# Moving loads and turns of u, v and z in the opening couples of a fused attention and maxout kernel

## The chip, the cores and the metric

The kernel runs on one core of one Trainium2 chip. A core has a matrix engine (TensorE, PE in the profile, with its weight loads as PEld), three more compute engines (VectorE or DVE, ScalarE or ACT, GpSimd or POOL), and SyncE (SP), which here only issues DMAs. Each engine runs its own queue of instructions in order, and they wait for one another through semaphores. The metric is the device time of one execution in microseconds (us), lower is better. Five executions of the kernel before took 918.5, 917.55, 910.27, 917.88 and 922.46 us; the median is 917.88.

## The reference: what is computed

There are 8 batches of 3072 positions. u and v have 256 columns, z has 64. The output of the first half, flattened to 24576 rows, feeds the second half:

```python
scores = (1.0 / S) * z @ z.T            # per batch, S = 3072
attn = np.maximum(scores, 0.0) ** 2
x = u * (attn @ v)
h1, h2 = x @ w1, x @ w2                 # 256 -> 1024
out = np.maximum(h1, h2) @ w_out        # 1024 -> 256
```

The scores are symmetric, so a block of them on one side of the diagonal is the transpose of a block on the other side.

## The kernel before

**Tiling.** A batch is cut into 6 groups of 512 positions (g), so its scores are 6 x 6 blocks of 512 x 512. Two groups make a couple (c = 0, 1, 2), and all couples of all batches are counted by i: couples 0 to 2 are batch 0, 3 to 5 are batch 1. v and z come in pieces of two groups, written v(batch, piece) and z(batch, piece); u comes by group, u(batch, group).

**Scores and their transposes.** `score_pair` computes a block in two halves: matmuls of zT (L211), a relu on ScalarE into r_sb (L224) and a square on VectorE (L230, L232). Blocks on the diagonal are computed as triangles and completed by three DMA transposes (L235). Blocks below the diagonal are made by `mirror`, one DMA transpose of a whole block (L263). During the steps of a couple the scores of the next couple are computed; the squares are issued 8 steps after their matmuls.

**Attention.** A couple is a list of steps, each with two matmuls of 64 rows that run side by side (L892). From couple 3 on it is a fast matrix product with 7 instead of 8 block products: VectorE forms S1, S2 and S3 of score blocks (L331, L335, L339, in `prepare`), S4 (L782), and combinations of v (`combine_v`, L171 to L174). Couple 2 is computed plainly. An accumulator that changes from one half of the array to the other needs a relay: a nop that waits for the last matmul of the old half and releases the first of the new one. In the plain couple relays are on GpSimd's queue, in the others on ScalarE's.

**Gate and feed-forward.** After the steps of couple i comes `second(i - 1)`: the feed-forward of the couple before (`ff`, L440 to L476), with tasks of VectorE hung between its matmuls: the gates of couple i (`gate`, L424, which reads uT), then S1, S2, S3 for couple i + 1. S2 is used from the first steps of the next couple, S3 from its step 12.

**Transfers.** `load_v`, `load_u` and `load_z` issue on GpSimd (L157, L183, L135) and cast to bf16. `turn_u` is a DMA transpose on SP (L187) of an un tile into uT; `turn_z` makes two copies on VectorE (L142) and a DMA transpose on SP into zT (L143). There are two buffers each of un, uT, zn and zd, so the third load of u must wait for the first turn. Five buffers hold v, so v(1,2) takes the buffer of v(0,2) and waits until couple 2, which reads v(0,2) first, is done with it after 32 steps. zT has four places; z(2,0) takes the one of z(0,2).

**Order of the work.** The program is written in order by hand. For each couple `plan` lists (step, what, batch, number). At that step the transfer is put into its engine's queue; a step is no time in itself, only a place in the order. At a step the relays come first, then squares that are due (with their triangles and mirrors), mirrors that are ready, scores, and then the entries of the plan. In the lists of couple 2:

```python
(1, turn_u, 0, 4), (2, load_v, 1, 0), (4, turn_u, 0, 5),
(6, load_v, 1, 1), (34, load_v, 1, 2),
```

Of the kernel before, what the change touches and what calls it, by code (L numbers as in the profile page):

```python
# [11 lines left out]
def kernel(  # L12
# [541 lines left out]
    with tc.manual_schedule():  # L554
# [185 lines left out]
        for i in range(PLAIN // 2, len(couples)):  # L740
# [98 lines left out]
            if i == 2:  # L839
                plan = [  # L840
                    (1, turn_u, 0, 4),
                    (2, load_v, 1, 0),
                    (4, turn_u, 0, 5),
                    (6, load_v, 1, 1),
                    (34, load_v, 1, 2),
                ]
            if i == 3:
                plan = [
                    (2, load_u, 1, 0),
                    (6, load_u, 1, 1),  # L850
                    (22, load_z, 2, 0),
                    (26, load_z, 2, 1),
                    (36, turn_u, 1, 0),
                    (42, turn_u, 1, 1),
                    (len(steps), load_u, 1, 2),
                    (len(steps), load_u, 1, 3),
                ]
            if i == 4:
                plan = [x for x in plan if x[1] not in (load_z, turn_z)] + [
                    (2, turn_z, 2, 0),  # L860
                    (10, turn_z, 2, 1),
                    (14, load_z, 2, 2),
                    (44, turn_z, 2, 2),
                ]
# [91 lines left out]
```

## Time and profile before

| | us |
|---|---|
| median of five executions | 917.88 |
| the profiled execution | 918.5 |
| its span, first to last instruction | 916.7 |
| TensorE busy | 901.5 |
| VectorE busy | 722.0 |
| ScalarE busy | 602.6 |
| GpSimd busy | 105.9 |

The mean granted clock of TensorE was 0.996 of full speed. The page of the profile gives busy times by engine, a picture of the span in 40 slices, the DMA queues and the chain of work that ended last. Further views answer for a stretch of time: the timeline of one engine, the waits (who waited for whom), and the busy times by stretch. A row of a timeline has start, duration, engine, line of the kernel, operation, output <- input, and how many of them were merged; in brackets stands the idle time before it and what ended it. "SPq" is the queue of SP; its duration is the time that a transfer's issue took there, not the transfer. Matmuls run in a pipeline, so their rows overlap.

### The profile page before, as it was taken

To read this page: it belongs to the slowest core of one execution; us is meant where nothing else is said; L and a number is where in the kernel's file an instruction comes from. 1 tells how busy PE (TensorE), PEld (TensorE's weight loads), DVE (VectorE), ACT (ScalarE), POOL (GpSimd) and SP (SyncE) were. 2 spreads that over 40 slices of the span, in tenths; PEclk is the share of its full clock that TensorE was granted. 3 is DMA by queue.
4 is the path that set the end of the run, shared out by engine and by line. 5 is a ranking of instruction groups with operands and counts; after the bars stand their busy time and mean duration, and the time that the engine had idled before them with its cause. 6 is when DMAs were issued, how large, how long until landed. Compare 5 with 4: busy or idle time off the path is not lost.

```text
span 916.7 us, 19227 instructions
## 1 busy us (share of the span) xinstructions
PE 901.5 (98%) x7478; PEld 520.1 (57%) x7526; DVE 722.0 (79%) x1091; ACT 602.6 (66%) x1193; POOL 105.9 (12%) x199
## 2 busy tenths in 40 slices
PE   8899999999999999999999999999989999999998
PEld 4356465665565655665646656556455564655655
DVE  6572689778997799887997979979789788995640
ACT  7687967567666676667676666666756667673445
POOL 4101010110101111101011012010110110100000
PEclk9899999999999999999999999999999999999999
DMA  9999978989798996999979999799999989987201
GB/s 182 174 190 187 196 160 143 188 164 192 142 177 156 158 202 113 202 149 180 170 127 205 148 159 182 144 193 155 154 154 133 189 159 182 166 161 149 74 24 70
DMA packets 381580, 145.60 MB, mean 159 GB/s; under 512 B 360240, under 2 KB 364720, under 8 KB 381488
## 3 DMA queue, kind: packets, MB, share of 16 engines
q1 hardware_dynamic: 359040, 91.79, 62.4%
q0 software_dynamic: 22448, 52.57, 30.9%
q8 instruction: 59, 0.97, 0.5%
q14 instruction: 33, 0.27, 0.1%
HBM read 59.77 MB, written 25.17 MB: 93 GB/s over the span
## 4 chain that ended last, share of the span: by engine, by line
PE 92%; DMA 3%; DVE 2%; issue 1%; ACT 1%; POOL 0%; ACTq 0%; DVEq 0%; POOLq 0%
PE acc L892 43%; PE o_ps L463 18%; PE d_ps L440 17%; PE s_ps L211 7%; PE o_ps L454 4%; PE acc L279 3%; DMA v_sb<-in_v_dram 2%; DMA blk<-blk 1%; DVE blk L232 1%; DMA uT<-un 0%; ACT r_sb L224 0%; PE acc L582 0%; DVE blk L335 0%; DVE blk L331 0%; PE w2o_ps L671 0%
## 5 line engine op out<-in xcount | busy, mean ns | idle before, releaser
L892 PE MATMUL acc<-blk,v_sb 64*128 64x512 bf16 x2208 | 451.3, 376 | 0.0
L224 ACT ACTIVATE r_sb<-s_ps 128x512 bf16<-128x512 f32 (+3 forms) x672 | 336.0, 559 | 128.1 <-PE s_ps L211 84.3
L892 PE MATMUL acc<-blk,vt 64*128 64x512 bf16 x1512 | 364.9, 376 | 2.5 <-DVE blk L335 2.3
L892 PEld LDWEIGHTS <-v_sb 64*128 64x128 bf16 x2208 | 176.2, 94 | 137.5 <-issue 10.0
L232 DVE TENSOR_TENSOR blk<-r_sb 128x1024 bf16<-128x1024 bf16 x257 | 172.7, 689 | 93.8 <-ACT r_sb L224 93.1
L447 ACT ACTIVATE g_sb<-d_ps 128x512 bf16<-128x512 f32 x384 | 193.3, 631 | 28.2 <-PE acc L892 17.8
L463 PE MATMUL o_ps<-w_out_sb,g_sb 128*128 128x256 bf16 x1536 | 175.5, 273 | 0.0
L892 PEld LDWEIGHTS <-vt 64*128 64x128 bf16 x1512 | 139.3, 94 | 62.7
L440 PE MATMUL d_ps<-xT,w_sb 128*128 128x512 bf16 x720 | 167.9, 380 | 2.8 <-ACT g_sb L447 0.2
L463 PEld LDWEIGHTS <-g_sb 128*128 128x128 bf16 x1536 | 150.3, 98 | 17.4
L475 ACT COPY o_sb<-o_ps 128x512 f32<-128x512 f32 (+1 forms) x98 | 56.3, 577 | 133.2 <-PE o_ps L463 131.5
L767 DVE TENSOR_TENSOR h_sb<-h_sb,acc 128x512 f32<-128x512 f32 x168 | 109.6, 684 | 28.3 <-ACT h_sb L771 20.9
L211 PE MATMUL s_ps<-zT 64*128 64x512 bf16 (+3 forms) x676 | 126.7, 359 | 0.7 <-ACT zT L129 0.4
L440 PEld LDWEIGHTS <-w_sb 128*128 128x128 bf16 x768 | 73.3, 98 | 89.8 <-issue 10.5
L476 POOL DMA_DIRECT2D out_dram<-o_sb x88 | 48.0, 546 | 524.4 <-ACT o_sb L475 524.4
L335 DVE TENSOR_TENSOR blk<-blk,blk 128x2048 bf16<-128x2048 bf16 x63 | 77.2, 1225 | 2.2
L331 DVE TENSOR_TENSOR blk<-blk,blk 128x2048 bf16<-128x2048 bf16 x63 | 76.8, 1220 | 0.0
L782 DVE TENSOR_TENSOR blk<-blk,blk 128x2048 bf16<-128x2048 bf16 x63 | 76.7, 1220 | 0.0
L339 DVE TENSOR_TENSOR blk<-blk,blk 128x2048 bf16<-128x2048 bf16 x63 | 73.3, 1220 | 4.1 <-DMA blk<-blk 4.1
L424 DVE SCALAR_TENSOR_TENSOR xT<-h_sb,uT 128x512 bf16<-128x512 f32 x96 | 62.1, 686 | 3.8 <-PE o_ps L454 3.8
L230 DVE TENSOR_TENSOR blk<-r_sb 128x512 bf16<-128x512 bf16 (+3 forms) x162 | 46.3, 324 | 19.9 <-ACT r_sb L224 18.9
L211 PEld LDWEIGHTS <-zT 64*128 64x128 bf16 x676 | 36.2, 95 | 38.6 <-DVE zT L129 0.9
(47 smaller groups left out, 317.5 us busy)
## 6 DMA issues: line engine op xcount, KB each, us to landing
out_dram<-o_sb POOLq DMA_DIRECT2D x88, 256.0 KB, 3.7
un<-in_u_dram POOLq DMA_DIRECT2D x48, 256.0 KB, 5.9
v_sb<-in_v_dram POOLq DMA_DIRECT2D x21, 512.0 KB, 7.7
blk<-blk SPq DMA_TRANSPOSE x240, 4.8
zn<-in_z_dram POOLq DMA_DIRECT2D x21, 128.0 KB, 4.8
v_sb<-in_v_dram POOLq DMA_DIRECT2D x6, 256.0 KB, 7.1
out_dram<-o_sb SPq DMA_DIRECT2D x6, 256.0 KB, 2.0
blk<-in_moe_w_dram POOLq DMA_DIRECT2D x2, 512.0 KB, 8.2
```

The lines of the kernel that those rows point to most:

```text
L211: nc.tensor.matmul(s_ps[h][:, lo[h] :], zT[rows, z_at(b, blk * G + tiles[h]), :], zT[rows, q + lo[h] // P : q + G, :].rearrange("p t c -> ...
L224: nc.scalar.activation(o, s, AF.Relu)
L232: nc.vector.tensor_mul(a[:, k : k + 2, :], r, r)
L331: nc.vector.tensor_add(*alike(f["S1"], f["A21"], f["A22"]))
L335: nc.vector.tensor_sub(*alike(f["S2"], f["S1"], f["A11"]))
L339: nc.vector.tensor_sub(*alike(f["S3"], f["A11"], f["A21"]))
L440: nc.tensor.matmul(d_ps, w15_sb[:, kc, ts(nb, P)], xT[:, kc, :], start=(kc == 0), stop=(kc == KD - 1),)
L447: nc.scalar.activation(g_sb[:, nb, :], d_ps, AF.Relu)
L463: nc.tensor.matmul(o_ps[t // 2][:, t % 2, :], g_sb[:, nb, ts(t, P)], w_out_sb[:, nb, :], start=False, stop=(nb == KF - 1 and t % 2 == 1),)
L767: nc.vector.tensor_add(out, a, b_)
L782: nc.vector.tensor_sub(f["A12"].ap, f["A12"].ap, f["S2"].ap)
L892: mm = nc.tensor.matmul(a.out(acc[name]), w()[rows], a.moving(rows, j), start=name not in opened, stop=left[name] == 0,)
```

## The change

Three lists of the plan are edited; nothing else. In couple 2 the three loads of v(1) move from steps 2, 6 and 34 to 12, 16 and 36. In couple 3 the loads of z(2,0) and z(2,1) move from steps 22 and 26 to 14 and 18, and the turns of u(1,0) and u(1,1) from 36 and 42 to 22 and 26. The turn of z(2,0) moves from step 2 of couple 4 to step 66 of couple 3. A couple of the fast kind has 84 steps, the plain one 96.

```diff
             if i == 2:
                 plan = [
                     (1, turn_u, 0, 4),
-                    (2, load_v, 1, 0),
                     (4, turn_u, 0, 5),
-                    (6, load_v, 1, 1),
-                    (34, load_v, 1, 2),
+                    (12, load_v, 1, 0),
+                    (16, load_v, 1, 1),
+                    (36, load_v, 1, 2),
                 ]
             if i == 3:
                 plan = [
                     (2, load_u, 1, 0),
                     (6, load_u, 1, 1),
-                    (22, load_z, 2, 0),
-                    (26, load_z, 2, 1),
-                    (36, turn_u, 1, 0),
-                    (42, turn_u, 1, 1),
+                    (14, load_z, 2, 0),
+                    (18, load_z, 2, 1),
+                    (22, turn_u, 1, 0),
+                    (26, turn_u, 1, 1),
+                    (66, turn_z, 2, 0),
                     (len(steps), load_u, 1, 2),
                     (len(steps), load_u, 1, 3),
                 ]
             if i == 4:
                 plan = [x for x in plan if x[1] not in (load_z, turn_z)] + [
-                    (2, turn_z, 2, 0),
                     (10, turn_z, 2, 1),
                     (14, load_z, 2, 2),
                     (44, turn_z, 2, 2),
```

## The prediction

> **What bounds the kernel now.** I began with the page. Its busy line says that TensorE works nearly all the time:
>
> ```profile
> PE 901.5 (98%) x7478; PEld 520.1 (57%) x7526; DVE 722.0 (79%) x1091; ACT 602.6 (66%) x1193; POOL 105.9 (12%) x199
> ```
>
> The chain that ended last agrees (PE 92%, DMA 3%). An average can hide a slow stage, so I cut the span at the first d_ps matmul of each feed-forward (the list of the chain gives 111.70, 148.55, 185.00 and so on) and asked for busy times by stretch. Columns: stretch, its length, busy us (and instructions) of PE, PEld, DVE, ACT, POOL, then the TensorE clock, DMA share, GB/s.
>
> ```profile
> 30.00:40.00 10.00, 6.51 (x56) 2.97 (x53) 6.52 (x12) 6.23 (x12) 1.81 (x3) 0.95 1.45 153
> 40.00:50.00 10.00, 9.97 (x68) 4.50 (x69) 4.20 (x8) 6.11 (x12) 0.00 (x0) 0.71 1.33 199
> ...
> 90.00:100.00 10.00, 10.00 (x96) 4.55 (x94) 6.03 (x9) 9.37 (x18) 0.53 (x1) 1.00 1.24 207
> ```
>
> ```profile
> 111.70:148.55 36.85, 36.74 (x307) 20.89 (x309) 34.20 (x54) 25.12 (x51) 4.87 (x9) 1.00 0.73 146
> 148.55:185.00 36.45, 36.35 (x306) 22.57 (x308) 30.94 (x53) 23.23 (x49) 4.86 (x9) 1.00 1.02 184
> ...
> 222.00:258.70 36.70, 36.59 (x307) 20.97 (x309) 34.81 (x59) 24.50 (x49) 4.33 (x8) 1.00 0.82 149
> 258.70:295.15 36.45, 36.34 (x307) 22.58 (x309) 30.37 (x50) 23.23 (x49) 4.35 (x8) 1.00 0.95 172
> ...
> 662.00:702.70 40.70, 38.10 (x309) 21.86 (x311) 35.40 (x59) 24.43 (x50) 4.34 (x8) 1.00 1.11 143
> ```
>
> The change edits couples 2, 3 and 4 (i = 2, 3, 4; some 86 to 185 us). Couple 2 runs from 85.7 to 111.7, x96 matmuls in the row 90:100 and as many in 100:110; the timeline there shows pairs of matmuls starting every 0.216 us without a gap. Couple 3, with the feed-forward before it, is 111.70:148.55, and couple 4 is 148.55:185.00. The same two couples of the next batch take 36.70 and 36.45. So couple 3 is 0.15 us over its twin, couple 4 is level, and I find no wait of TensorE between 72 and 662 us over 0.4 us. What is lost at all is lost elsewhere: near 35 us (3.5 us idle, then a clock of 0.71) and at 662:702 (4.0 us over its twin, 36.70). The change touches neither. **The gain open to it in this execution is about 0.2 us.** The question is what it can spoil.
>
> **The queues that it reorders.** A step number orders an instruction only within its own engine's queue. SP's queue (start, time in the queue, line, transfer), couple 3 and the end of it:
>
> ```profile
> 136.00 4.45 SPq L235 DMA_TRANSPOSE blk<-blk  x3
> 140.54 1.45 SPq L187 DMA_TRANSPOSE uT<-un  x1
> 142.08 3.78 SPq L235 DMA_TRANSPOSE blk<-blk  x3
> 146.38 3.09 SPq L263 DMA_TRANSPOSE blk<-blk  x1
> 149.57 1.25 SPq L187 DMA_TRANSPOSE uT<-un  x1
> 150.92 10.71 SPq L263 DMA_TRANSPOSE blk<-blk  x3
> ```
>
> L235 are the triangles, L263 the mirrors, L187 the turns of u. GpSimd's queue:
>
> ```profile
> 87.24 1.10 POOL L157 DMA_DIRECT2D v_sb<-in_v_dram  x2
> 95.58 0.53 POOL L157 DMA_DIRECT2D v_sb<-in_v_dram  x1 [7.24 <-PE s_ps L211]
> 128.72 1.10 POOL L183 DMA_DIRECT2D un<-in_u_dram  x2
> 129.78 1.10 POOL L135 DMA_DIRECT2D zn<-in_z_dram  x2
> 144.49 0.53 POOL L183 DMA_DIRECT2D un<-in_u_dram  x1 [13.60 <-DMA uT<-un]
> 153.40 0.53 POOL L183 DMA_DIRECT2D un<-in_u_dram  x1 [8.38 <-DMA uT<-un]
> ```
>
> And VectorE, which consumes what they bring:
>
> ```profile
> 154.03 1.28 DVE L424 SCALAR_TENSOR_TENSOR xT<-h_sb,uT 128x512 bf16<-128x512 f32 x2
> 155.23 1.22 DVE L331 TENSOR_TENSOR blk<-blk,blk 128x2048 bf16<-128x2048 bf16 x1
> ...
> 161.25 3.50 DVE L339 TENSOR_TENSOR blk<-blk,blk 128x2048 bf16<-128x2048 bf16 x3 [1.15 <-DMA blk<-blk]
> 164.67 0.49 DVE L142 COPY zd<-zn 128x512 bf16<-128x512 bf16 x2
> ```
>
> **Part 1, loads of v(1) later in couple 2.** In this plain couple the relays ("half done" nops) sit on GpSimd's queue and wait for TensorE, so here a step number is a time. Step 0 starts at 85.67; four steps and a score pair take 1.08 us. Relays of step 12 wait for the end of step 11, about 88.9; the load follows, so v(1,0) goes out near 89.0 instead of 87.24 and v(1,1) near 90.1 instead of 87.79; v(1,2) near 96.6 instead of 95.58. Before, they landed 7.5 to 9.6 us after issue, the last at about 103.6. The first reader is L171 at 118.0 on VectorE. With the slowest landing of any v in this trace (14.0 us) the last would land at 110.6. Nobody is late. A load holds GpSimd 0.53 to 0.55 us, the next relays come four steps (0.9 to 1.1 us) later and are needed another four steps on: no wait is added. The Trainium skill speaks against this part: "DMA: Bandwidth & Descriptors", Rules for kernel authors, says to issue a transfer early and wait for it late. If its cover were gone, later issue would cost what it is later, 1.0 to 2.3 us; by the row, with more than 7 us of cover left, 0. I take 0. What is gained, that the turns of u(0,4) and u(0,5) do not share their time with v (they landed in 10.5 and 12.2 us here, against 3.1 to 3.4 in couple 3), ends at 103.1 and is read by L424 at 113.2: also 0.
>
> **Part 2, loads of z(2) from 22, 26 to 14, 18.** GpSimd's order is u, u, z, z before and after, with nothing of couple 3 between (its relays are on ScalarE). The rows show z issued at 129.78, long before step 22 (132.7). No change: 0.
>
> **Part 3, turns of u(1,0), u(1,1) from 36, 42 to 22, 26.** Each costs SP 1.25 to 1.45 us of queue. The mirror of block (2,3) is emitted at step 15 and runs 132.68 to 135.9; the first triangle is emitted at 27, the second at 39. So the turns pass both triangles and one mirror. The loads of u land 4.6 to 5.4 us after 128.7, by 134.7, before SP comes free, so the turns do not block it. New order: turns 136.0 to 138.8, first triangle 138.8 to 143.2 (2.8 us later), second 143.2 to 147.1 (1.3 later), mirrors from there as before or 0.5 earlier, since the turn at 149.57 is gone. Who waits for triangles: S1 of the own blocks, L331 at 155.23. The second triangle's last piece landed by 149.3 (issue 144.6 plus 4.7), now by 150.6; cover shrinks from 5.9 to 4.6 us. Cost 0. Gain: uT(1,1) landed at 152.9 for a gate at 154.03, a cover of 1.15 us that becomes some 12; the third and fourth loads of u, held at 144.49 and 153.40 until a turn freed a buffer, go out near 140 and 141.5, in the stretch 140:150, where the DMA share is 0.69. Nothing waited there, so 0.
>
> **Part 4, turn of z(2,0) from step 2 of couple 4 to step 66 of couple 3.** Two copies of 287 ns leave VectorE at 164.67 (0.49 us together) and come near 144.5, where it is busy without a break; one transpose (1.3 us of SP) passes the mirrors flushed at the couple's end. The mirrors issued from 152.92 on move 0.7 us back; the last to matter landed at 161.25, when the first S3 (L339) began. TensorE uses S3 from step 12 of couple 4, 166.9, while the first L339 ends at 162.5: 4.4 us of cover, 4.2 for the third. Copies plus transpose eat 0.5 to 1.2 of it. The other end of VectorE's 0.49: ScalarE had already waited 1.38 us on L232 at 143.3 (three buffers of r_sb), so a score could be late by up to 0.5; TensorE showed nothing of the 1.38, so I take 0 and keep +0.5. In return the zT of batch 2, landed 170.9 and first read at 174.3, gains 20 us of cover.
>
> **Sum.** Against the profiled execution, 918.5 us (span 916.7 and 1.8 around it): parts 0, 0, 0 and 0, within -0.2 and +0.5; about 918.4. The median of the five runs, 917.88, lies 0.6 below that execution, so **917.8**.
>
> **Rivals.**
> A, all of it is hidden: 917.8, chance 0.88. That part of the change does nothing (the loads of z) belongs here.
> B, slower: the mirrors behind the moved turn of z land too late for S3. It decides when they slip by more than 4.2 us beyond 161.25. For: SP's transposes can swell, a turn in couple 2 held the queue 5.56 us and landed in 10.5 to 12.2. With u and z swollen so, the slip is 7.1 (10.5 - 3.4) + 1.3 - 4.2 = 4.2 us of stall. Then the clock: the Trainium skill ("TensorE: Matmul & The Clock Gate", Part 1: The HAM clock gate) says an idle window of about 3.4 us halves the clock and about as much busy time restores it, so 1.7 us more. The row says worse: 0.71 over 40:50 is 5.8 us at half, 2.9 us lost. By the rule 923.7, by the row 924.9; I use the row. Against: in 130 to 150 the DMAs land in 2.3 to 5.7 us and the share is under 0.9. Chance 0.08, half of it over 1% only with a disturbance on top.
> C, faster: the thin covers (1.15 us of uT, 3.4 of zT) are overdrawn in other executions than the one profiled, or the stretch 662:702 falls differently with shifted transfers. Worth up to 4.0 there, and 3.5 + 2.9 if the early stall went too: 911.5 to 914. Against: the change is far from both places. Chance 0.04.
>
> **Range and chances.** The runs before spread from 910.27 to 922.46, so a median of a few may move by 3 or 4 us unprovoked; 1% (9.2 us) is about what a measurement can tell from no change. 911.5 (C) to 924.0 (most of B). Faster 0.03, same 0.92, slower 0.05.
>
> **What would show it.** v_sb issues at 89, 90 and 96.6; the z loads still right behind u near 130; SP with two L187 ahead of the first L235, and L143 before the last L263s; first L235 2.8 us later; uT gates unhindered; stages still 36.7 and 36.45. I am wrong if TensorE waits for L335 or L339 near 164 to 170 us, for zT, or if the clock falls below 1.00 after 86 us.

## The result, and the profile after

The change moves nothing that can be measured: the ratio of after to before is **1.0004, 95% interval 0.9980 to 1.0028**. The medians are 919.89 us over 43 executions after (910.56 to 939.75) and 922.26 us over 80 executions before (909.8 to 948.82). The ratio compares only the executions within 1.5% of the fastest of each kernel and the medians take all of them, which is why the two do not agree to the last 0.3%.

The profiled execution after took 920.89 us, its span is 919.1. Busy times by stretch, cut at the start of the first d_ps matmul of each feed-forward, 0.44 us ahead of the marks in the prediction, which leaves the lengths as they are (stretch, length, busy us and instructions of PE, PEld, DVE, ACT, POOL, then TensorE clock, DMA share, GB/s). The rows are couple 2, couple 3, couple 4, and the first couple of batch 4:

```profile
64.32:114.06 49.74, 44.12 (x349) 22.72 (x348) 17.94 (x29) 35.24 (x68) 4.90 (x9) 0.93 1.18 192
114.06:150.92 36.86, 36.76 (x309) 20.91 (x309) 34.28 (x56) 25.57 (x52) 5.40 (x10) 1.00 0.78 142
150.92:187.37 36.45, 36.35 (x308) 22.56 (x309) 30.44 (x51) 23.23 (x49) 4.33 (x8) 1.00 0.95 176
444.66:484.40 39.74, 37.63 (x309) 21.63 (x309) 34.90 (x58) 24.29 (x49) 4.35 (x8) 1.00 1.12 149
```

Couples 3 and 4, which hold five of the eight moved entries, take 36.86 and 36.45 us, what they took before within 0.01 us. Couple 2 took 49.74 where an execution without a wait takes 41.97 (below). TensorE's timeline there shows the reason:

```profile
86.77 0.38 PE L211 MATMUL s_ps<-zT 64*128 64x512 bf16 x2
86.98 1.03 PE L892 MATMUL acc<-blk,v_sb 64*128 64x512 bf16 x8
93.32 0.61 PE L211 MATMUL s_ps<-zT 64*128 64x512 bf16 x2 [5.31 <-DMA zT<-zd]
```

A score of batch 1 waited 5.31 us for a turn of z(1), and the clock fell for a while (0.93 over the stretch). That turn is not one of those moved. Its transpose came late to SP, behind a mirror:

```profile
73.87 9.50 SPq L263 DMA_TRANSPOSE blk<-blk  x1
83.46 2.41 SPq L143 DMA_TRANSPOSE zT<-zd  x1
```

It went out 19.1 us after the mark of the feed-forward; in an execution without a wait (sp_only, below) it was 12.0. The obvious suspect is the change itself, which puts the loads of v beside these turns later. But a kernel whose program up to couple 3 is that of before (z20_late, below) waited at the same place:

```profile
91.96 0.61 PE L211 MATMUL s_ps<-zT 64*128 64x512 bf16 x2 [4.52 <-DMA zT<-zd]
```

There the turn had reached SP after 12.6 us, hardly later than in sp_only, and was late all the same. The first couple of batch 4 has the other loss, 39.74 us where 36.68 is the time without a wait: VectorE waits for v, as it did near 662 us in the profile before. Its waits over 447 to 485 us:

```profile
DVE vt L171 <- DMA v_sb<-in_v_dram: 3.1, 1, 3.1
```

SP's queue after, couple 3 and the end of it (start, time in the queue):

```profile
138.94 2.64 SPq L187 DMA_TRANSPOSE uT<-un  x2
141.67 9.07 SPq L235 DMA_TRANSPOSE blk<-blk  x6
150.84 7.58 SPq L263 DMA_TRANSPOSE blk<-blk  x3
158.53 1.93 SPq L143 DMA_TRANSPOSE zT<-zd  x1
160.55 3.92 SPq L263 DMA_TRANSPOSE blk<-blk  x1
```

Both turns of u stand ahead of both triangles. The turn of z (L143) passes one mirror; three of the four that follow the triangles are still ahead of it. GpSimd's queue:

```profile
84.82 0.54 POOL L157 DMA_DIRECT2D v_sb<-in_v_dram  x1 [2.53 <-PE s_ps L211]
85.90 0.54 POOL L157 DMA_DIRECT2D v_sb<-in_v_dram  x1 [0.54 <-PE acc L892]
98.90 0.53 POOL L157 DMA_DIRECT2D v_sb<-in_v_dram  x1 [12.45 <-PE s_ps L211]
...
131.54 1.10 POOL L183 DMA_DIRECT2D un<-in_u_dram  x2
132.60 1.10 POOL L135 DMA_DIRECT2D zn<-in_z_dram  x2
144.34 0.53 POOL L183 DMA_DIRECT2D un<-in_u_dram  x1 [10.64 <-DMA uT<-un]
146.05 0.53 POOL L183 DMA_DIRECT2D un<-in_u_dram  x1 [1.17 <-DMA uT<-un]
```

The loads of v now wait for TensorE through the relays; the loads of z(2) follow u at once, exactly as before; the third and fourth loads of u lie 1.7 us apart instead of 8.9.

### The profile page after: what moved, and what is told of

It is laid out like the page before. It is cut to its first block, busy times and chain, and to the rows that moved or that the text cites. A ratio compares the mean times of both kernels' runs of the same rounds, so it can differ in the third digit from the quotient of the medians.

```text
span 919.1 us, 19229 instructions
## 1 busy us (share of the span) xinstructions
PE 901.7 (98%) x7478; PEld 520.3 (57%) x7526; DVE 721.7 (79%) x1091; ACT 602.4 (66%) x1193; POOL 105.4 (11%) x199
## 4 chain that ended last, share of the span: by engine, by line
PE 90%; DMA 5%; DVE 2%; issue 2%; ACT 1%; POOL 0%; ACTq 0%; POOLq 0%; DVEq 0%
PE acc L892 42%; PE o_ps L463 17%; PE d_ps L440 17%; PE s_ps L211 6%; PE o_ps L454 4%; PE acc L279 2%; DMA v_sb<-in_v_dram 1%; DMA zT<-zd 1%; DMA zn<-in_z_dram 1%; DMA blk<-blk 1%; DVE blk L232 0%; DMA uT<-un 0%; PE acc L582 0%; ACT r_sb L224 0%; DVE blk L335 0%
## 5 line engine op out<-in xcount | busy, mean ns | idle before, releaser
L331 DVE TENSOR_TENSOR blk<-blk,blk 128x2048 bf16<-128x2048 bf16 x63 | 76.9, 1220 | 0.4 <-DMA blk<-blk 0.4
L339 DVE TENSOR_TENSOR blk<-blk,blk 128x2048 bf16<-128x2048 bf16 x63 | 73.3, 1219 | 0.0
```

Source lines behind the costliest of these rows:

```text
L331: nc.vector.tensor_add(*alike(f["S1"], f["A21"], f["A22"]))
L339: nc.vector.tensor_sub(*alike(f["S3"], f["A11"], f["A21"]))
```

## The experiments

Two theories. **Hidden:** every moved transfer has cover, so the change is worth nothing, and what an execution takes above 908 us comes from other transfers that happen to land late. **Cancelling:** one half of the change gains and the other half loses. Beside these stands the prediction's slower rival, with a threshold of 4.2 us for the mirrors that S3 waits for. Some kernels below have a line more, so their line numbers are one or a few higher.

### One half at a time

```diff
 v_only: the kernel before, with
-(2, load_v, 1, 0), (6, load_v, 1, 1), (34, load_v, 1, 2)
+(12, load_v, 1, 0), (16, load_v, 1, 1), (36, load_v, 1, 2)
 sp_only: the changed kernel, with those three lines put back
```

> Only the three loads of v(1) are moved (12, 16, 36); couples 3 and 4 as before. If all parts are hidden: ratio to the kernel before 1.000 within 0.4%, couple 3 with its feed-forward 36.86 us and couple 4 36.45 us, first L171 of v(1) not waiting for a transfer. If the two halves of the change cancel: this half is off 1.000 by more than 0.4% one way, and the half with the turns by as much the other way.

> Only the turns of u and z (and the loads of z, whose place in GpSimd's queue does not change) are moved; the loads of v(1) as before. If hidden: 1.000 within 0.4%, stages of couples 3 and 4 36.86 and 36.45 us, first triangle on SP's queue about 2.8 us later than before, counted from the start of couple 3. If the halves cancel: off 1.000 by more than 0.4%.

Measured: v_only 1.0014 (0.9947 to 1.0081), sp_only 0.9968 (0.9921 to 1.0015). Both intervals contain 1, so there is no sign of two halves that cancel, though with these intervals a pair of 0.3% each would not be seen. The profiles say more. That of sp_only happened to have hardly any wait: its span is 908.2 us, and its rows for couples 2, 3 and 4 are the nominal times of all later comparisons:

```profile
64.19:106.16 41.97, 41.76 (x351) 22.25 (x348) 17.93 (x29) 35.23 (x68) 4.92 (x9) 1.00 1.16 191
106.16:143.02 36.86, 36.86 (x311) 20.90 (x309) 34.27 (x56) 25.58 (x52) 5.40 (x10) 1.00 0.94 172
143.02:179.47 36.45, 36.45 (x310) 22.56 (x309) 30.43 (x51) 23.24 (x49) 4.34 (x8) 1.00 0.97 172
```

In v_only couple 4 took 39.31 us. TensorE's waits in it:

```profile
161.81 0.37 PE L211 MATMUL s_ps<-zT 64*128 64x512 bf16 x1 [0.53 <-ACT o_sb L475]
169.84 0.39 PE L211 MATMUL s_ps<-zT 64*128 64x512 bf16 x2 [0.63 <-DMA zT<-zd]
179.60 0.39 PE L211 MATMUL s_ps<-zT 64*128 64x512 bf16 x2 [1.07 <-DMA zT<-zd]
```

The second row is the first score of batch 2. Here the turn of z(2,0) stood at its old place (step 2 of couple 4), went out at 164.60 and came too late by 0.63 us. So the cover of 3.4 us that I read from one execution can be used up in another. The first score of batch 2 waited in none of the profiles with the moved turn, except under the dose below. The third row waits for z(2,1), which the change leaves where it was.

The other thin cover, 1.15 us of uT(1,1) before its gate, was overdrawn here too. VectorE's timeline:

```profile
152.94 1.29 DVE L424 SCALAR_TENSOR_TENSOR xT<-h_sb,uT 128x512 bf16<-128x512 f32 x2 [3.51 <-DMA uT<-un]
```

Of the three profiles with the turns of u at their old places, this one and z20_late (3.65 us) have the wait and that of before has not; the nine with the moved turns and no dose on them do not have it. So the change does remove a wait of VectorE. As far as the profiles show it is worth nothing: TensorE did not wait for VectorE in couple 4 of either execution.

### The cover of the loads of v

```diff
-(12, load_v, 1, 0), (16, load_v, 1, 1), (36, load_v, 1, 2)
+(len(steps), load_v, 1, 0), (len(steps), load_v, 1, 1), (len(steps), load_v, 1, 2)
```

> The changed kernel, with all three loads of v(1) put at the end of couple 2 (step 96 in place of 12, 16, 36), about 22 us later than in the change. This measures the cover that I gave the loads: issue at the first d_ps of the feed-forward, landing 7.5 to 10 us later, first reader L171 only 6.3 us after that d_ps. If the cover is what I said: VectorE waits 1 to 4 us for v at L171, the third S2 slips past its 1.3 us of cover, and couple 3 with its feed-forward takes 37 to 40 us in place of 36.86 (ratio 1.000 to 1.004). If loads of v there matter through the transfers beside them and not through their own landing: zT of batch 1, which the scores of couple 2 read, lands faster than the 9.8 to 12.2 us seen so far, and couple 2 shows no wait for it.

Measured: issue at 111.00 to 112.1, which is 15 to 20 us later than in the change (counted from the feed-forward's start and without the wait in couple 2), landing a median of 10.0 us after issue. VectorE's timeline, first reader of v(1):

```profile
121.51 0.42 DVE L171 TENSOR_TENSOR vt<-v_sb 128x512 bf16<-128x512 bf16 x1 [2.50 <-DMA v_sb<-in_v_dram]
```

and couple 3 took 38.76 us, 1.90 over nominal. This execution was the longest of the twelve, and the ratio, 0.9964 (0.9922 to 1.0005), shows no loss; the cost is read from this one stage. There a delay of 15 to 20 us uses up the cover and costs 1.9 us; the change's delay of 0.5 to 3.1 us costs none (couple 3 is nominal in v_only). The second half of the expectation fell: without any load of v beside it, zT of batch 1 was still late in couple 2 (a wait of 4.60 us). So that turn can be late without the loads of v.

### The dose for the slower rival

```diff
 def turn_z(b, piece, times=1):
+    for _ in range(times):        # the transpose alone
         nc.sync.dma_start_transpose(...)
-(66, turn_z, 2, 0)
+(66, turn_z, 2, 0, 4)
```

> The changed kernel, with every transpose of the moved turn of z(2,0) issued four times in a row at step 66 (same source, same place, so the result is unchanged). This is the dose for the slower rival: three more transposes of at least 1.3 us each on SP's queue ahead of the last mirrors of couple 3, up to 5 us each if every one waits for the one before it to land. If the cover of S3 is 4.2 us, as the slower rival has it: with 3.9 us more the first L339 starts later but TensorE waits under 0.5 us; with 12 us or more TensorE waits 5 us or longer near the start of couple 4 and couple 4 takes 41 us or more in place of 36.45. If the mirrors at the end are not what S3 waits for: L339 stays where it is, and couple 4 at 36.45.

Measured, SP's queue:

```profile
143.27 7.64 SPq L264 DMA_TRANSPOSE blk<-blk  x3
151.01 13.74 SPq L144 DMA_TRANSPOSE zT<-zd  x4
164.84 5.03 SPq L264 DMA_TRANSPOSE blk<-blk  x1
```

The turn held the queue for 13.74 us instead of 1.9, and the mirror behind it went out 12 us later. VectorE's S3:

```profile
154.98 3.49 DVE L340 TENSOR_TENSOR blk<-blk,blk 128x2048 bf16<-128x2048 bf16 x3
```

S3 (L339, here L340) started before that mirror was even issued and waited for nothing. The rival as I placed it is refuted: no mirror that S3 needs stands behind the turn of z. Couple 4 did take 39.48 us, but from the dose itself: the first score of batch 2 waited 2.33 us for the last of the repeated transposes, which write what it reads. The ratio, 1.0101 (0.9967 to 1.0235) from four runs, tells nothing alone.

### The dose for the triangles

```diff
 def turn_u(b, g, times=1):
+    for _ in range(times):        # the transpose alone
         nc.sync.dma_start_transpose(...)
-(26, turn_u, 1, 1)
+(26, turn_u, 1, 1, 4)
```

> The changed kernel, with the transpose of u(1,1) issued four times in a row at step 26 (same source and place, so the result is unchanged). The dose for the triangles: three more transposes on SP's queue ahead of both triangles, 1.3 us each if none waits, 3.4 to 4.5 us each if every one waits for the one before it to land. With my cover of 4.6 us between the second triangle and the S1 of the own blocks: at 3.9 us more VectorE waits under 1 us for a triangle; at 10 to 13 us more it waits 5 to 9 us at L331, and TensorE, which has some 4 us of cover behind that, waits 1 to 5 us near the start of couple 4 (36.45 us becomes 37.5 to 42). If triangles are not what S1 waits for: no wait at L331.

Measured, SP's queue and then VectorE:

```profile
133.73 15.91 SPq L188 DMA_TRANSPOSE uT<-un  x5
149.76 8.55 SPq L236 DMA_TRANSPOSE blk<-blk  x6
158.36 13.96 SPq L264 DMA_TRANSPOSE blk<-blk  x3
```

```profile
160.09 1.22 DVE L332 TENSOR_TENSOR blk<-blk,blk 128x2048 bf16<-128x2048 bf16 x1 [6.49 <-DMA blk<-blk]
...
174.42 1.23 DVE L340 TENSOR_TENSOR blk<-blk,blk 128x2048 bf16<-128x2048 bf16 x1 [9.45 <-DMA blk<-blk]
```

The last triangle left SP's queue 15.4 us later than in sp_only (both counted from the first d_ps of their feed-forward: 158.31 - 106.28 = 52.03 against 142.81 - 106.16 = 36.65), and S1 started 9.8 us later than in the changed kernel (53.8 against 158.04 - 114.06 = 44.0). The cover that the changed kernel has left is thus 15.4 - 9.8 = 5.6 us in these profiles, where I had 4.6. (Only 6.49 of the 9.8 us are the wait shown; 3.16 are a wait of the gate before it for the repeated turn.) Beyond it the price was higher than expected: the mirrors queue behind the triangles, so S3 waited another 9.45 us, and TensorE waited 12.2 us in three pieces:

```profile
162.62 0.37 PE L893 MATMUL acc<-blk,vt 64*128 64x512 bf16 x1 [2.27 <-DVE blk L336]
165.02 0.58 PE L893 MATMUL acc<-blk,vt 64*128 64x512 bf16 x1 [1.12 <-DVE blk L336]
175.70 0.58 PE L893 MATMUL acc<-blk,vt 64*128 64x512 bf16 x1 [8.82 <-DVE blk L340]
```

Couple 4 took 52.74 us, 16.3 over nominal. Ratio 1.0215 (1.0132 to 1.0297), from two runs. So a slower outcome exists, but on the triangles' side: the triangles would have to slip by more than 5.6 us beyond where the change has already put them.

### The turn of z(2,0) the other way

```diff
-(2, turn_z, 2, 0), (10, turn_z, 2, 1)
+(10, turn_z, 2, 1), (24, turn_z, 2, 0)
```

This is an edit of the kernel before.

> The kernel before, with its turn of z(2,0) at step 24 of couple 4 instead of 2, behind the turn of z(2,1) and one mirror. I counted 3.4 us of cover between the landing of that turn and the first score of batch 2. If that is right: TensorE waits for zT at step 37 of couple 4, 2 us (if SP comes to it 5.9 us later) to 9 us (if it also stands behind the mirror), and couple 4 takes 38.5 to 48 us in place of 36.45. If the place of this turn is free, as the change's sum has it for the move the other way: no wait, 36.45.

Measured, TensorE in couple 4:

```profile
188.18 0.61 PE L211 MATMUL s_ps<-zT 64*128 64x512 bf16 x2 [14.49 <-DMA zT<-zd]
```

A wait of 14.49 us, more than the 9 expected: the mirror ahead of it held SP for 7.15 us, the turn went out at 180.34 and took another 7.8 us to land. Couple 4 took 53.92 us; ratio 1.0145 (1.0056 to 1.0234), from two runs. A late turn of z is expensive in this execution, so its place is worth nothing only on the early side.

### Where the rest of the time goes

> The changed kernel once more, on the chip of the next three. If the change moves nothing: ratio 1.000 within 0.4%, couples 3 and 4 at 36.86 and 36.45 us again, and the time above the 908 us of an execution without stalls sits in the opening, in couple 2 (a wait for zT of batch 1) or in the stage of a first couple of a later batch, in no fixed one of them.

Measured: 1.0016 (0.9976 to 1.0057); the profiled span was 911.4 us, couples 2, 3 and 4 were nominal, and 2.9 us were lost in the first couple of batch 2, with VectorE waiting 2.9 us for v at L171.

I then cut every profile at the same places and subtracted the stage times of sp_only. What is left (us; "first couples" are those of batches 2 to 7):

| profile | span | opening | couple 2 | couple 3 | couple 4 | first couples | other |
|---|---|---|---|---|---|---|---|
| before | 916.7 | 5.1 | 0 | 0 | 0 | 3.5 | 0.2 |
| after | 919.1 | 0.1 | 7.8 | 0 | 0 | 3.1 | 0.2 |
| after_again | 911.4 | 0 | 0 | 0 | 0 | 2.9 | 0.4 |
| v_only | 915.8 | 0.4 | 0 | 0 | 2.9 | 4.4 | 0 |
| z_dose | 916.9 | 0 | 0 | 0 | 3.0 | 5.8 | 0 |
| v_end | 924.5 | -0.4 | 6.5 | 1.9 | 0 | 8.4 | 0 |
| u_dose | 931.6 | 0.1 | 0 | 0 | 16.3 | 6.3 | 0.9 |
| z20_late | 931.4 | -0.5 | 6.2 | 0 | 17.5 | 0 | 0 |
| z1_early | 910.1 | 0.5 | 0 | 0 | 0 | 1.5 | 0 |
| z1_again | 920.9 | 0.8 | 0 | 0 | 6.2 | 5.8 | 0 |
| v0_late | 914.4 | 0.1 | 0 | 0 | 0 | 1.9 | 4.2 |
| both | 907.7 | -0.4 | 0 | 0 | 0 | 0 | 0 |

In these profiles everything above 908 us lies in a few stages, and the waits that were looked up in these stages lead back to late transfers. It comes and goes between executions of one kernel (compare after and after_again, or z1_early and z1_again, which are the same kernels). The longest executions, up to 950 us of the kernel before, were not profiled; that they are made of the same waits is not shown. The last four rows are those of two edits that were to widen the two covers that fail most:

```diff
 z1_early (on the changed kernel): group 3 of the opening
-if (i, n) == (3, 14): load_z(1, 2, held=True)
+if (i, n) == (3, 2): load_z(1, 2, held=True)
+if (i, n) == (3, 1): turn_z(1, 1)
+if (i, n) == (3, 14): turn_z(1, 2)          # both out of the tasks of the first feed-forward
 v0_late (on the changed kernel): prepared(), where a batch begins
-tasks = gates[:KD] + first + gates[KD:] + tasks + sum(others, [])
+tasks = gates[:KD] + first + gates[KD:]
 ...
+tasks += sides[1] + sides[2] + others[0] + sides[0] + others[1]
```

> The changed kernel with the turns of z(1,1) and z(1,2) put earlier: z(1,1) from the feed-forward of couple 0 to group 3, ahead of the last two mirrors of batch 0, z(1,2) right behind these mirrors, its load from n = 14 to n = 2 of group 3. If the wait of couple 2 for zT (5.3 us of wait, 7.8 us of stage, in the profile of the changed kernel; none in that of before) is one of the late transfers that set the level: couple 2 with its feed-forward stays at 41.97 us, and the median falls by what such stalls cost on average, 1 to 3 us (ratio 0.997 to 0.999). If the level is set elsewhere: ratio 1.000.

> The changed kernel with VectorE's four combinations of v(b+1,0) put behind those of v(b+1,2) and one pair of S1 and S2, in the feed-forward ahead of every first couple of a batch: 1.7 + 2.45 = 4.2 us more cover for the load that is issued last. If late loads of v(b+1,0) set the level: no first L171 waits for v(b+1,0), the stages of first couples stay at 36.68 us, and the median falls by 2 to 5 us (ratio 0.995 to 0.998). If it is the clock or the chip: the excess stays, ratio 1.000.

> Both of the last two edits on the changed kernel. If late transfers at these two places set the level: the gains add, 3 to 7 us (ratio 0.992 to 0.997), with a median near 912 to 918. If not: 1.000.

> The kernel with the turns of z(1,1) and z(1,2) put earlier, a second time on this chip, since 14 runs left an interval of 0.9944 to 1.0031. If the wait of couple 2 for zT is one of the stalls that set the level: again no wait for zT in couple 2, couple 2 at 41.97 us, ratio 0.996 to 0.999. If its share is too small to measure: ratio 1.000 within 0.3%.

Measured: z1_early 0.9987 (0.9944 to 1.0031), again 0.9992 (0.9955 to 1.0029); v0_late 0.9979 (0.9941 to 1.0017); both 0.9996 (0.9961 to 1.0031). All hold 1: the expected gains of 0.1 to 0.8% are not shown, and no version here is measured to beat the two kernels. The medians of all executions do move the expected way: 914.13 us (z1_early), 916.2 (v0_late) and 916.48 (both) against 921.51 for the unedited changed kernel and 923.34 for the kernel before on the same chip, but on another chip 919.13 (z1_again) against 921.49. Whether these edits make long executions rarer is open. In the profiles, couple 2 was nominal in all three profiles with the earlier turns (z1_early, both, z1_again), but it was also nominal in seven of the ten without them. z1_again lost 6.2 us in couple 4, where TensorE waited 4.45 us for z(2,1). In v0_late VectorE still waited 2.0 us for v and, in the stages around it, 7.0 and 4.9 us for transposes of blocks at L339 and L331. A wider cover at one place leaves the other thin places, and at this size the ratio can't tell them. What makes single transfers late, and why in one execution and not in the next, stays open.

## Why the prediction was right or wrong

- **The step that failed is the base of the sum:** "The median of the five runs, 917.88, lies 0.6 below that execution, so **917.8**." 80 executions of the same kernel have a median of 922.26, and three later sets 922.92, 923.34 and 921.49, so the base was 4.4 us too low. Measured from there, 917.8 says a gain of 4.5 us, which no part of the sum contains. It was the draw of a few executions: 27 of the 80 are at or below 917.88, so five of them with a median so low are no rare thing. The base did hold waits for late transfers, 8.8 us of them in the one profiled execution; but the table above has from 3.3 to 11.2 us of them in profiles of the two kernels, and I gave no term to how far they would differ elsewhere. I had met them (near 35 us and near 662) and put them aside: "The change touches neither." That is true of the difference and false of the level. My range named the spread, "3 or 4 us unprovoked"; the number did not use it.
- **The change is worth nothing: right, for the difference.** The sum had -0.1 us, between -0.2 and +0.5; the interval of the ratio is -1.8 to +2.6 us around +0.4. The 0.2 us that I counted as open are no wait: couple 3 takes 36.86 us in sp_only too.
- **The sign of being wrong was drawn too wide.** I wrote that I am wrong if TensorE waits "for zT, or if the clock falls below 1.00 after 86 us". Both happened in the profile after, at 93 us, and the kernel z20_late did the same with the loads of v where they were before. The sign should have named z(2,0), the turn that is moved.
- **Part 1, v later: right, sizes off.** From the profiles of v_only and sp_only, counted from the feed-forward's start, the loads went out 2.5, 3.1 and 0.5 us later; I had 1.8, 2.3 and 1.0. The advice of the Trainium skill to issue early ("DMA: Bandwidth & Descriptors", Rules for kernel authors) did not matter at this distance; at 15 to 20 us (v_end) it did, by 1.9 us.
- **Part 2, loads of z: right.** Same order on GpSimd, issue directly behind u.
- **Part 3, turns of u: right, in part by luck.** The two turns hold SP for 2.64 us ahead of the triangles, predicted 2.8. The first L235 went out 27.61 us after the first d_ps of the feed-forward against 24.75 before, which looks like the same number; but with the old order it went out at 27.01 in v_only and 27.17 in z20_late, so between executions this place moves by as much. Cover 5.6 us by the dose, predicted 4.6.
- **Part 4, turn of z(2,0): zero is right, the working is not.** I wrote that "The mirrors issued from 152.92 on move 0.7 us back". Only one mirror stands behind the turn, and S3 does not wait for that one. I had placed the mirrors by the time at which they ran instead of by the step that emits them: SP ran behind, and three of the four mirrors had been emitted before step 66. For the same reason the turn itself reached SP 10.9 us after its copies (147.6 to 158.53) and its cover grew from 3.4 to 13.3 us, not by 20 (landing 5.3 us after issue, first read at 177.1).
- **Rival B** had the right kind of mechanism at the wrong place. With the swelling that it supposed, S3 would not have moved. **Rival C** was right that the thin covers are overdrawn in other executions (0.63 us of zT, 3.5 of uT), but no run here measures a gain from it.
- **The clock after a wait.** For rival B I weighed 1.7 us (an estimate from the rule in the Trainium skill, "TensorE: Matmul & The Clock Gate", Part 1: The HAM clock gate) against 2.9 us (a row of before) and used the row. Stage excess less wait gives 7.8 - 5.3 = 2.5 (after), 6.5 - 4.6 = 1.9 (v_end), 6.2 - 4.45 = 1.7 (z1_again) and 17.5 - 14.5 = 3.0 (z20_late): from the one to the other, and not proportional to the wait. The "3.5 us idle" of that row are several pieces; the longest wait there is 2.9 us, for a transpose.

## What to carry to other kernels

A step number in a hand-written plan is a place in one queue: list what stands between the old and the new place on that engine, and in which order it was emitted, before any time is put on the move. When the bounding engine shows no gap in the edited stages, price the cover of every moved transfer, and test it with a dose, since a profile of the change alone can't show how much was left. Keep the difference and the level apart: cut several profiles at the same marks, and take the level from many executions.

## What the runs showed of the hardware that was not expected

- Loads of one kind can land at very different times: those of v_sb took 5.2 to 14.0 us in the profile before (median 7.5) and 5.1 to 18.6 us in that of v0_late (median 8.0).
- Four transposes in a row to the same place held SP's queue for 13.74 us where one took 1.9: the later ones waited for the earlier to land (7.1 us of SP's waits are on zT).
- Waits of TensorE of about 1 us (0.53, 0.63 and 1.07 us in v_only) left the granted clock at 1.00; with one of 5.31 us it was 0.93 over its stage. In u_dose it fell early: after the wait of 2.27 us, and ahead of the one of 8.82, it was 0.73 over 162.62 to 165.00 and 0.50 from 165 to 180, where a matmul took 0.63 us instead of 0.38. Yet the wait of 2.33 us in z_dose left no such mark: its length alone does not tell.
